# A mixture-of-state kernel on one Trainium2 core: contracting the first product over 256 (head, state) rows

## The chip, the cores and the metric

The kernel runs on one core of one Trainium2 chip. The metric is the device time of one execution in microseconds (us), median over several runs; for the kernel before it is 1129.18 us (three runs, 1129.02 to 1129.24). Besides, one execution was recorded by the hardware profiler, and all durations below come from that one.

## The reference, cut to what matters

Inputs are `x` (8 batches, 8 heads, 512 tokens, 64 features), `state` (8 batches, 8 heads, 32 states, 64 features), both in float32, and `w_in` (512 x 2048) and `w_out` (2048 x 512), both in float64. The output is float32.

```python
scores = scale * x @ state.T                 # per batch and head: 512 x 32
a      = softmax(scores, over the 32 states)
xread  = a @ state                           # 512 x 64
a2     = softmax(scores.T, over the 512 tokens)
sread  = a2 @ x                              # 32 x 64
rows   = concat([xread, sread], over tokens) # 8*544 rows of 8*64 = 512 features
h      = rows @ w_in                         # 4352 x 2048
out    = (h * erf(softplus(h))) @ w_out      # 4352 x 512
```

So a token's row before the first product is `xread`, for each head a weighted mean of that head's 32 states; the rows of the states themselves (`sread`, 32 for each batch) follow the tokens of their batch.

## The kernel before, in words

The work runs batch by batch. A batch has 512 tokens, and the hidden dimension of 2048 is cut into four groups g of 512 (`NG` = 4, each of `GF` = 4 tiles of 128). For each batch and group the kernel calls

- `hidden` (L219 to L236): for each of the four 128-wide tiles of the group, four matmuls (L230, k over the four 128-row blocks of the 512 features) accumulate `h` transposed, 128 x 512, in one of two PSUM buffers (`ps_h`); ScalarE writes softplus of it into `s` (L232), VectorE copies it into `hs` (L233); when all four are there ScalarE takes erf of `s` (L234) and VectorE multiplies with `hs` into `gT` (L235).
- `project` (L238 to L244): 16 matmuls (L241) add the group's share of the second product into four PSUM accumulators (`ps_o`), which after the last group are copied out by ScalarE (L249) and stored.

`project` of a group is called after `hidden` of the next one (`pending`). In the program every f32 matmul stands in the trace as two instructions, a transposing one as one.

`attention(b, hb, xx)` (L131 to L217) prepares the tokens of batch b for half of the heads (four heads in `hb`, in two pairs j). It is called twice for each batch, during the batch before it, after groups 1 and 3; for batch 0 it is called ahead of everything. Per half: the state block `st` is transposed (L136) to `stT`; x is transposed, 8 matmuls (L144), to `xT`; the token scores, 8 matmuls of 64 columns (L152); a softmax over states (L158 to L167, VectorE with an exp on ScalarE at L162); the state scores, two matmuls whose 64 output rows lie side by side in one PSUM bank (L173); a softmax over tokens (L177 to L185, exp at L181); both weights transposed back (L189, L196) and copied by ScalarE; `xread` transposed, two matmuls of 64 contraction rows each (L204), copied into `xx` (L206), which `hidden` reads; `sread`, 8 matmuls of 64 columns (L212), copied into `sT` (L216). All PSUM tiles of attention share two buffers (`ps_at`). `st` holds each head's 64 features in one half of 128 columns and zeros in the other.

After the eight batches a ninth chunk takes the 256 state rows from `sT` through the same `hidden` and `project`.

The weights arrive as float64 and are turned into float32 by VectorE (`weight`, L84 to L113): 16 chunks of 128 x 1024 elements, seven VectorE instructions each, the raw words in the two buffers of the tag `hs` that `hidden` uses as well, loaded by SyncE's DMA queue (L93). `weights(g)` is called ahead of `hidden(0, g)`, so the conversion runs during batch 0.

No order is written out by hand beyond this: a scheduler places each engine's instructions by priority (the order of the program) and readiness by its own estimates, so that matmuls of `hidden` and `project` are put between the steps of `attention`. Each engine then runs its own list strictly in that order.

Of the kernel before, what the change touches and what calls it, by code (L numbers as in the profile page):

```python
# [8 lines left out]
F32 = mybir.dt.float32  # L9
# [7 lines left out]
def kernel(  # L17
# [7 lines left out]
):  # L25
    nc = tc.nc
# [3 lines left out]
    P = 128  # L30
    QH = 4
    NH = H // QH
# [7 lines left out]
    assert QH * Ns == P and 2 * D == P and d_model == H * D and S == 512  # L40
# [3 lines left out]
    xin = ctx.enter_context(tc.tile_pool(name="xin", bufs=3))  # L44
    att = ctx.enter_context(tc.tile_pool(name="att", bufs=1))
    small = ctx.enter_context(tc.tile_pool(name="small", bufs=2))
    xmid = ctx.enter_context(tc.tile_pool(name="xmid", bufs=2))
    act = ctx.enter_context(tc.tile_pool(name="act", bufs=2))
    act1 = ctx.enter_context(tc.tile_pool(name="act1", bufs=1))
# [8 lines left out]


    st = const.tile([P, NH, B, 2 * D], F32, name="st")  # L60
    nc.vector.memset(st, 0.0)

# [3 lines left out]
    def load_x(b, hb):  # L66
        t = xin.tile([P, NC, QH, D], F32, name="x")
        for q in range(QH):
            nc.sync.dma_start(out=t[:, :, q, :],  # L69
                              in_=x[b, QH * hb + q].rearrange("(p c) d -> p c d", c=NC))  # L70
        x_t[b, hb] = t

    load_x(0, 0)
    for hb in range(NH):
        for q in range(QH):
            nc.sync.dma_start(
                out=st[Ns * q:Ns * q + Ns, hb, :, D * (q % 2):D * (q % 2) + D],
                in_=state[:, QH * hb + q].rearrange("b n d -> n b d"))
    load_x(0, 1)
# [4 lines left out]
    def weight(dst, src, shape):  # L84
# [12 lines left out]
        e = act.tile([P, n], U32, name="u")  # L97
# [7 lines left out]
        m = act.tile([P, n], U32, name="s")  # L105
        nc.vector.tensor_scalar(m, hi, 0xFFFFF, 0x100000, op0=ALU.bitwise_and,
                                op1=ALU.bitwise_or)
        f = act1.tile([P, n], F32, name="w")
# [8 lines left out]
    def weights(g):  # L117
        fs = slice(gw * g, gw * g + gw)
        for k in range(0, NK, 2):
            weight(w_in[:, k:k + 2, fs],  # L120
                   moe_w_in[P * k:P * k + 2 * P, fs].rearrange("(k p) f -> p k f", p=P),
                   (2, gw))
        for t in range(GF * g, GF * g + GF, 2):
            weight(w_out[:, t:t + 2, :],
                   moe_w_out[P * t:P * t + 2 * P].rearrange("(t p) e -> p t e", p=P),
                   (2, d_model))


    sT = const.tile([P, NK, B, Ns], F32, name="sT")

    def attention(b, hb, xx):  # L131

        xt = x_t.pop((b, hb))

        stT_ps = ps_at.tile([P, P], F32, name="at")
        nc.tensor.transpose(out=stT_ps, in_=st[:, hb, b, :], identity=ident)  # L136
        stT = small.tile([P, P], F32, name="stT")
        nc.scalar.copy(stT, stT_ps)  # L138

        xT = att.tile([P, 2, S], F32, name="xT")  # L140
        for j in range(2):
            xp = ps_at.tile([P, S], F32, name="at")
            for c in range(NC):
                nc.tensor.transpose(out=xp[:, P * c:P * c + P],  # L144
                                    in_=xt[:, c, 2 * j:2 * j + 2, :], identity=ident)
            nc.scalar.copy(xT[:, j, :], xp)  # L146


        s1 = ps_at.tile([P, NC, QH, Ns], F32, name="at")
        for c in range(NC):  # L150
            for j in range(2):
                nc.tensor.matmul(out=s1[:, c, 2 * j:2 * j + 2, :],  # L152
                                 lhsT=xT[:, j, P * c:P * c + P],
                                 rhs=stT[:, 2 * Ns * j:2 * Ns * j + 2 * Ns],
                                 start=True, stop=True)
        s1v = s1.rearrange("p c q n -> p (c q) n")
        m1 = small.tile([P, NC * QH], F32, name="m1")
        nc.vector.reduce_max(out=m1, in_=s1v, axis=AX.X)  # L158
        a = att.tile([P, NC * QH, Ns], F32, name="a")
        nc.vector.tensor_tensor(a, s1v, m1.unsqueeze(2).to_broadcast([P, NC * QH, Ns]),  # L160
                                op=ALU.subtract)
        nc.scalar.activation(out=a, in_=a, func=ACTF.Exp, scale=scale)  # L162
        z1 = small.tile([P, NC * QH], F32, name="z1")
        nc.vector.reduce_sum(out=z1, in_=a, axis=AX.X)
        nc.vector.tensor_scalar(z1, z1, 1e-9, None, op0=ALU.add)
        nc.vector.reciprocal(z1, z1)
        nc.vector.tensor_tensor(a, a, z1.unsqueeze(2).to_broadcast([P, NC * QH, Ns]),  # L167
                                op=ALU.mult)


        s2 = ps_at.tile([P, S], F32, name="at")
        for j in range(2):
            nc.tensor.matmul(out=s2[D * j:D * j + D, :],  # L173
                             lhsT=stT[:, 2 * Ns * j:2 * Ns * j + 2 * Ns],
                             rhs=xT[:, j, :], start=True, stop=True)
        m2 = small.tile([P, 1], F32, name="m2")
        nc.vector.reduce_max(out=m2, in_=s2, axis=AX.X)  # L177
        nc.vector.tensor_scalar(m2, m2, -scale, None, op0=ALU.mult)
        a2 = att.tile([P, S], F32, name="a2")
        z2 = small.tile([P, 1], F32, name="z2")  # L180
        nc.scalar.activation(out=a2, in_=s2, func=ACTF.Exp, bias=m2, scale=scale,  # L181
                             accum_out=z2)
        nc.vector.tensor_scalar(z2, z2, 1e-9, None, op0=ALU.add)
        nc.vector.reciprocal(z2, z2)
        nc.vector.tensor_scalar(a2, a2, z2, None, op0=ALU.mult)  # L185

        aT_ps = ps_at.tile([P, S], F32, name="at")
        for c in range(NC):
            nc.tensor.transpose(out=aT_ps[:, P * c:P * c + P],  # L189
                                in_=a[:, QH * c:QH * c + QH, :], identity=ident)  # L190
        aT = att.tile([P, S], F32, name="aT")
        nc.scalar.copy(aT, aT_ps)  # L192

        a2T_ps = ps_at.tile([P, NC, P], F32, name="at")
        for c in range(NC):
            nc.tensor.transpose(out=a2T_ps[:, c, :], in_=a2[:, P * c:P * c + P],  # L196
                                identity=ident)
        a2T = att.tile([P, NC, P], F32, name="a2T")
        nc.scalar.copy(a2T, a2T_ps)

        for j in range(2):
            rows = slice(2 * Ns * j, 2 * Ns * j + 2 * Ns)
            y = ps_at.tile([P, S], F32, name="at")
            nc.tensor.matmul(out=y, lhsT=st[rows, hb, b, :], rhs=aT[rows, :],  # L204
                             start=True, stop=True)
            nc.scalar.copy(xx[:, 2 * hb + j, :], y)  # L206


        sr = ps_at.tile([P, 2, 2 * Ns], F32, name="at")
        for j in range(2):  # L210
            for c in range(NC):
                nc.tensor.matmul(out=sr[:, j, :], lhsT=xt[:, c, 2 * j:2 * j + 2, :],  # L212
                                 rhs=a2T[:, c, 2 * Ns * j:2 * Ns * j + 2 * Ns],
                                 start=(c == 0), stop=(c == NC - 1))
        for e in range(2):
            nc.scalar.copy(sT[D * e:D * e + D, 2 * hb:2 * hb + 2, b, :],  # L216
                           sr[D * e:D * e + D, :, Ns * e:Ns * e + Ns])  # L217

    def hidden(xx, n, g):  # L219

        hs = act.tile([P, GF, S], F32, name="hs")[:, :, 0:n]
        s = act.tile([P, GF, S], F32, name="s")[:, :, 0:n]
        gT = act.tile([P, GF, S], F32, name="gT")[:, :, 0:n]
        for i in range(GF):
            f0 = P * (GF * g + i)
            hp = ps_h.tile([P, S], F32, name="h")
            for k in range(NK):
                nc.tensor.matmul(out=hp[:, 0:n], lhsT=w_in[:, k, f0:f0 + P], rhs=xx[:, k, :],  # L230
                                 start=(k == 0), stop=(k == NK - 1))
            nc.scalar.activation(out=s[:, i, :], in_=hp[:, 0:n], func=ACTF.Softplus)  # L232
            nc.vector.tensor_copy(hs[:, i, :], hp[:, 0:n])  # L233
        nc.scalar.activation(out=s, in_=s, func=ACTF.Erf)  # L234
        nc.vector.tensor_tensor(gT, s, hs, op=ALU.mult)  # L235
        return gT  # L236
# [28 lines left out]
    def new_xx():  # L265
        return xmid.tile([P, NK, S], F32, name="xx")

    xx = new_xx()
    for hb in range(NH):
        attention(0, hb, xx)  # L270

    chunks = [(S, put_x(b)) for b in range(B)] + [(B * Ns, put_s)]
    pending = None
    for b, (n, put) in enumerate(chunks):
        nxt = new_xx() if b + 1 < B else None
        cur = xx if b < B else sT.rearrange("p k b n -> p k (b n)")
        acc = None
        for g in range(NG):
            if b + 1 < B and g % 2 == 0:
                load_x(b + 1, g // 2)  # L280
            if b == 0:
                weights(g)
            gT = hidden(cur, n, g)
# [9 lines left out]
            if b + 1 < B and g % 2 == 1:  # L293
                attention(b + 1, g // 2, nxt)
        xx = nxt
# [31 lines left out]
```

## Time and profile before

| what | us |
|---|---|
| median of three runs | 1129.18 |
| the profiled execution's own time | 1126.09 |
| its span, first to last instruction | 1124.3 |
| TensorE matmuls busy | 1084.4 |
| ScalarE busy, table loads included | 365.4 |
| VectorE busy | 334.7 |
| mean granted TensorE clock | 0.985 |

The page gives, for each engine, the time in which an instruction was running and its share of the span; then the chain of work that ended last, followed back from the last instruction. Each piece of the chain belongs to the engine and line that everything later waited for. A busy TensorE can be one that runs short matmuls in a row, so the length of a stretch and the count of matmuls in it are read together. In the names of rows, `128*64 128x512` is a matmul with 128 contraction rows, 64 output rows and 512 columns. PE is TensorE, PEld its weight loads, DVE VectorE, ACT ScalarE, SP SyncE.

### The profile page before, as it was taken

To read this page: it belongs to the slowest core of one execution; us is meant where nothing else is said; L and a number is where in the kernel's file an instruction comes from. 1 tells how busy PE (TensorE), PEld (TensorE's weight loads), DVE (VectorE), ACT (ScalarE), POOL (GpSimd) and SP (SyncE) were. 2 spreads that over 40 slices of the span, in tenths; PEclk is the share of its full clock that TensorE was granted. 3 is DMA by queue.
4 is the path that set the end of the run, shared out by engine and by line. 5 is a ranking of instruction groups with operands and counts; after the bars stand their busy time and mean duration, and the time that the engine had idled before them with its cause. 6 is when DMAs were issued, how large, how long until landed. Compare 5 with 4: busy or idle time off the path is not lost.

```text
span 1124.3 us, 7665 instructions
## 1 busy us (share of the span) xinstructions
PE 1084.4 (96%) x3152; PEld 530.1 (47%) x3152; DVE 334.7 (30%) x469; ACT 365.4 (33%) x494; POOL 0.7 (0%) x6
## 2 busy tenths in 40 slices
PE   6779999999999999999999999999999999999998
PEld 4434444454444445454444445454444445444564
DVE  2888873221222212221211312221211311211111
ACT  2143214432342413432342413432342413322242
POOL 0000000000000000000000000000000000000000
PEclk9589999999999999999999999999999999999999
DMA  5333331000010001000010001000000000000000
GB/s 162 100 112 129 117 109 29 29 19 1 1 56 1 19 1 29 28 15 5 0 57 0 20 1 29 28 4 15 1 35 3 1 0 10 29 0 1 19 19 19
DMA packets 45346, 35.09 MB, mean 31 GB/s; under 512 B 36864, under 2 KB 36864, under 8 KB 45312
## 3 DMA queue, kind: packets, MB, share of 16 engines
q1 hardware_dynamic: 45312, 34.61, 10.1%
q8 instruction: 25, 0.41, 0.2%
q14 instruction: 9, 0.07, 0.0%
HBM read 25.69 MB, written 8.91 MB: 31 GB/s over the span
## 4 chain that ended last, share of the span: by engine, by line
PE 94%; DVE 2%; ACT 2%; DMA 1%; SPq 0%; issue 0%; ACTq 0%
PE h L230 42%; PE o L241 41%; PE at L212 3%; PE at L152 3%; PE at L204 2%; PE at L144 2%; PE at L173 1%; ACT xx L206 1%; PE at L196 1%; PE at L189 1%; DMA hs<-in_moe_w_in_dram 0%; ACT s L234 0%; DVE u L102 0%; ACT L234 0%; SPq L69 0%
## 5 line engine op out<-in xcount | busy, mean ns | idle before, releaser
L241 PE MATMUL o<-w_out,gT 128*128 128x512 f32 x1088 | 477.6, 592 | 0.7 <-DVE gT L235 0.7
L230 PE MATMUL h<-xx,w_in 128*128 128x512 f32 x1024 | 460.1, 600 | 6.7 <-DVE w_in L111 6.6
L241 PEld LDWEIGHTS o<-w_out,gT 128*128 128x128 f32 x1088 | 206.1, 190 | 254.5 <-issue 252.6
L230 PEld LDWEIGHTS h<-xx,w_in 128*128 128x128 f32 x1024 | 192.3, 192 | 243.3 <-issue 230.0
L233 DVE COPY hs<-h 128x512 f32<-128x512 f32 (+1 forms) x144 | 95.2, 661 | 518.0 <-ACT s L232 518.0
L232 ACT ACTIVATE s<-h 128x512 f32<-128x512 f32 (+1 forms) x144 | 82.2, 573 | 403.9 <-PE h L230 403.5
L235 DVE TENSOR_TENSOR gT<-s,hs 128x2048 f32<-128x2048 f32 (+1 forms) x36 | 78.2, 2173 | 78.6 <-ACT s L234 78.6
L234 ACT ACTIVATE s<-s 128x2048 f32<-128x2048 f32 (+1 forms) x36 | 65.3, 1815 | 0.4
L232 ACT ACT_TABLE_LOAD x37 | 47.5, 1283 | 42.1 <-DVE w L109 41.5
L158 DVE TENSOR_REDUCE m<-at 128x16 f32<-128x512 f32 x16 | 11.1, 691 | 160.0 <-PE at L152 160.0
L138 ACT COPY stT<-at 128x128 f32<-128x128 f32 x16 | 4.2, 265 | 131.9 <-PE at L136 131.8
L234 ACT ACT_TABLE_LOAD x36 | 46.2, 1283 | 0.6
L212 PE MATMUL at<-a2T,x 128*128 128x64 f32 x256 | 33.6, 287 | 9.2 <-ACT xx L206 9.2
L212 PEld LDWEIGHTS at<-a2T,x 128*128 128x128 f32 x256 | 31.4, 200 | 23.4 <-ACT xx L206 23.4
L152 PEld LDWEIGHTS at<-stT,xT 128*128 128x128 f32 x256 | 34.3, 209 | 8.3 <-ACT xT L146 5.4
L152 PE MATMUL at<-stT,xT 128*128 128x64 f32 x256 | 34.9, 292 | 0.6 <-ACT xT L146 0.5
L249 ACT COPY ot<-o 128x512 f32<-128x512 f32 x34 | 19.8, 582 | 45.9 <-PE o L241 45.9
L230 PE MATMUL h<-sT,w_in 128*128 128x256 f32 x128 | 28.9, 379 | 0.0
L230 PEld LDWEIGHTS h<-sT,w_in 128*128 128x128 f32 x128 | 24.3, 190 | 6.7 <-issue 3.8
L192 ACT COPY aT<-at 128x512 f32<-128x512 f32 x16 | 9.4, 585 | 42.1 <-PE at L189 42.1
L204 PE MATMUL at<-aT,st 64*128 64x512 f32 x64 | 21.5, 694 | 0.9 <-ACT aT L192 0.9
L144 PE MATMUL at<-ident,x 128*128 128x128 f32 x128 | 20.6, 297 | 1.3 <-ACT stT L138 0.9
(44 smaller groups left out, 354.4 us busy)
## 6 DMA issues: line engine op xcount, KB each, us to landing
x<-in_x_dram SPq DMA_DIRECT2D x64, 128.0 KB, 2.9
hs<-in_moe_w_in_dram SPq DMA_DIRECT2D x8, 1024.0 KB, 5.3
hs<-in_moe_w_out_dram SPq DMA_DIRECT2D x8, 1024.0 KB, 4.9
out_dram<-ot SPq DMA_DIRECT2D x32, 256.0 KB, 2.2
st<-in_state_dram SPq DMA_DIRECT2D x8, 64.0 KB, 2.3
out_dram<-ot SPq DMA_DIRECT2D x8, 64.0 KB, 1.7
```

The source lines that it names most:

```text
L144: nc.tensor.transpose(out=xp[:, P * c:P * c + P], in_=xt[:, c, 2 * j:2 * j + 2, :], identity=ident)
L152: nc.tensor.matmul(out=s1[:, c, 2 * j:2 * j + 2, :], lhsT=xT[:, j, P * c:P * c + P], rhs=stT[:, 2 * Ns * j:2 * Ns * j + 2 * Ns], start=Tru ...
L173: nc.tensor.matmul(out=s2[D * j:D * j + D, :], lhsT=stT[:, 2 * Ns * j:2 * Ns * j + 2 * Ns], rhs=xT[:, j, :], start=True, stop=True)
L204: nc.tensor.matmul(out=y, lhsT=st[rows, hb, b, :], rhs=aT[rows, :], start=True, stop=True)
L212: nc.tensor.matmul(out=sr[:, j, :], lhsT=xt[:, c, 2 * j:2 * j + 2, :], rhs=a2T[:, c, 2 * Ns * j:2 * Ns * j + 2 * Ns], start=(c == 0), stop ...
L230: nc.tensor.matmul(out=hp[:, 0:n], lhsT=w_in[:, k, f0:f0 + P], rhs=xx[:, k, :], start=(k == 0), stop=(k == NK - 1))
L232: nc.scalar.activation(out=s[:, i, :], in_=hp[:, 0:n], func=ACTF.Softplus)
L233: nc.vector.tensor_copy(hs[:, i, :], hp[:, 0:n])
L234: nc.scalar.activation(out=s, in_=s, func=ACTF.Erf)
L235: nc.vector.tensor_tensor(gT, s, hs, op=ALU.mult)
L241: nc.tensor.matmul(out=acc[r], lhsT=gT[:, i, P * r:P * r + P], rhs=w_out[:, GF * g + i, :], start=(g == 0 and i == 0), stop=(g == NG - 1 a ...
L249: nc.scalar.copy(ot, acc[r])
```

## The change

A token's row is a (weights over states) times state, so the first product can be written as a times (state @ w_in): per batch there are 8 x 32 = 256 rows (head, state) of state @ w_in, and `hidden` contracts over those 256 rows in place of the 512 features.

- `mixed(b, g)` is new: it makes the 256 x 512 block of state @ w_in of a batch and group, as eight matmuls of 64 contraction rows (one head's features), 32 output rows (its states) and 512 columns. The heads with even number (e = 0) use the contraction rows 0 to 63 and one PSUM bank, the odd ones rows 64 to 127 and the other bank; the four pairs i lie in different 32-row strips of the bank. One half is copied out by ScalarE and one by VectorE. It is called for batch b + 1 after each group of batch b, for batch 0 right after the group's `w_in`.
- `hidden` takes a list of pairs: two matmuls per tile for the tokens (`mg`, `aT`), four as before for the state rows.
- `attention(b)` is called once for each batch, after group 1, for all eight heads. The state scores are eight matmuls laid out like those of `mixed`; ScalarE copies them out, and the token scores are made from them by eight transposes in place of the matmuls of L152. The matmuls of L204 and the copies into `xx` are gone: `aT` is what `hidden` reads. `sread` is 32 matmuls with 32 output rows and 64 columns, its normalisation moved behind it, and one more transpose puts it into `sT`.
- `st` has no zero halves any more and isn't cleared; x of a batch is loaded with eight DMAs at group 0; the state's DMAs come after all of x of batch 0.
- `weight` works in one tile of the tag `s` (three buffers, before two) for its two temporaries, and `hidden` writes its product over `s`; the tags `u`, `w`, `gT` and the `xx` buffers are gone. `weights(g)` is split, with `mixed(0, g)` between the halves.

```diff
-    def attention(b, hb, xx):
+    def states(b):
+        ps = ps_at.tile([P, P], F32, name="at")
+        nc.tensor.transpose(out=ps, in_=st[:, b, :], identity=ident)
+        stT[b] = keep.tile([P, P], F32, name="stT")
+        nc.scalar.copy(stT[b], ps)
+
+    def attention(b):
+        xt = x_t.pop(b)
...
+        s2 = [ps_at.tile([P, S], F32, name="at") for _ in range(2)]
+        for i in range(NI):
+            for e in range(2):
+                r, q = slice(D * e, D * e + D), slice(Ns * i, Ns * i + Ns)
+                nc.tensor.matmul(out=s2[e][q, :], lhsT=stT[b][r, q], rhs=xT[r, i, :],
                                  start=True, stop=True)
...
+        sc = att.tile([P, 2, S], F32, name="sc")
+        for e in range(2):
+            nc.scalar.copy(sc[:, e], s2[e])
...
+            s1 = ps_at.tile([P, NC * NI, Ns], F32, name="at")
+            for c in range(NC):
+                nc.tensor.transpose(out=s1[:, NI * c:NI * c + NI, :],
+                                    in_=sc[:, e, P * c:P * c + P], identity=ident)
...
-        for j in range(2):
-            rows = slice(2 * Ns * j, 2 * Ns * j + 2 * Ns)
-            y = ps_at.tile([P, S], F32, name="at")
-            nc.tensor.matmul(out=y, lhsT=st[rows, hb, b, :], rhs=aT[rows, :],
-                             start=True, stop=True)
-            nc.scalar.copy(xx[:, 2 * hb + j, :], y)
...
+        sr = ps_at.tile([P, 2, D], F32, name="at")
+        for e in range(2):
+            for c in range(NC):
+                for i in range(NI):
+                    q = slice(Ns * i, Ns * i + Ns)
+                    nc.tensor.matmul(out=sr[q, e, :], lhsT=a2T[:, e, c, q],
+                                     rhs=xt[:, c, 2 * i + e, :],
+                                     start=(c == 0), stop=(c == NC - 1))
...
+    def mixed(b, g):
+        mg = mix.tile([P, 2, gw], F32, name="m")
+        ps = [ps_at.tile([P, gw], F32, name="at") for _ in range(2)]
+        for i in range(NI):
+            for e in range(2):
+                r, q = slice(D * e, D * e + D), slice(Ns * i, Ns * i + Ns)
+                nc.tensor.matmul(out=ps[e][q, :], lhsT=stT[b][r, q],
+                                 rhs=w_in[r, i, gw * g:gw * g + gw], start=True, stop=True)
+        nc.scalar.copy(mg[:, 0], ps[0])
+        nc.vector.tensor_copy(mg[:, 1], ps[1])
+        m_t[b, g] = mg
...
-            for k in range(NK):
-                nc.tensor.matmul(out=hp[:, 0:n], lhsT=w_in[:, k, f0:f0 + P], rhs=xx[:, k, :],
-                                 start=(k == 0), stop=(k == NK - 1))
+            for k, (lhsT, rhs) in enumerate(pairs):
+                nc.tensor.matmul(out=hp[:, 0:n], lhsT=lhsT[:, P * i:P * i + P], rhs=rhs,
+                                 start=(k == 0), stop=(k == len(pairs) - 1))
...
-            if b + 1 < B and g % 2 == 0:
-                load_x(b + 1, g // 2)
             if b == 0:
-                weights(g)
-            gT = hidden(cur, n, g)
+                weights_in(g)
+                mixed(0, g)
+                weights_out(g)
+            if b + 1 < B and g == 0:
+                load_x(b + 1)
+                states(b + 1)
+            gT = hidden(pairs(b, g), n)
...
-            if b + 1 < B and g % 2 == 1:
-                attention(b + 1, g // 2, nxt)
+            if b + 1 < B:
+                mixed(b + 1, g)
+                if g == 1:
+                    attention(b + 1)
```

More of the change, by code (lines that the diff above doesn't have):

```diff
@@ L30 @@
     P = 128
-    QH = 4
-    NH = H // QH
+    NI = H // 2
     NC = S // P
@@ L56, with load_x @@
     make_identity(nc, ident)
-    st = const.tile([P, NH, B, 2 * D], F32, name="st")
-    nc.vector.memset(st, 0.0)
     x_t = {}
[L66 to L79, printed above, removed]
+    def load_x(b):
+        t = xin.tile([P, NC, H, D], F32, name="x")
+        for h in range(H):
+            nc.sync.dma_start(out=t[:, :, h, :], in_=x[b, h].rearrange("(p c) d -> p c d", c=NC))
+        x_t[b] = t
+    load_x(0)
+    st = const.tile([P, B, P], F32, name="st")
+    for h in range(H):
+        i, e = h // 2, h % 2
+        nc.sync.dma_start(out=st[Ns * i:Ns * i + Ns, :, D * e:D * e + D],
+                          in_=state[:, h].rearrange("b n d -> n b d"))
     w_in = const.tile([P, NK, d_ff], F32, name="w_in")
@@ L95, in weight @@
         lo, hi = words[:, :, 0], words[:, :, 1]
-        e = act.tile([P, n], U32, name="u")
+        em = act.tile([P, 2, n], U32, name="s", bufs=3)
+        e, m = em[:, 0], em[:, 1]
         nc.vector.tensor_scalar(e, hi, 20, 0x7FF, op0=ALU.logical_shift_right,
@@ L115, with weights_in @@
     gw = GF * P
-    def weights(g):
+    def weights_in(g):
         fs = slice(gw * g, gw * g + gw)
@@ L129 @@
     sT = const.tile([P, NK, B, Ns], F32, name="sT")
-    def attention(b, hb, xx):
[L133 to L140, printed above, removed]
-        for j in range(2):
+    stT = {}
+    aT = {}
+    def states(b):
[3 more added lines that the diff above has]
+        nc.scalar.copy(stT[b], ps)
@@ L142, in attention @@
+    def attention(b):
+        xt = x_t.pop(b)
+        xT = att.tile([P, NI, S], F32, name="xT")
+        for i in range(NI):
             xp = ps_at.tile([P, S], F32, name="at")
             for c in range(NC):
[L144 to L154, printed above, removed]
-                                 start=True, stop=True)
@@ L156, in attention @@
[L156 to L182, printed above, removed]
+                nc.tensor.transpose(out=xp[:, P * c:P * c + P], in_=xt[:, c, 2 * i:2 * i + 2, :],
+                                    identity=ident)
@@ new lines, in attention @@
+        a = att.tile([P, 2, NC * NI, Ns], F32, name="a")
+        a2 = att.tile([P, 2, S], F32, name="a2")
+        a2T = att.tile([P, 2, NC, P], F32, name="a2T")
+        aT[b] = keep.tile([P, 2, S], F32, name="aT")
+        z2 = small.tile([P, 2], F32, name="z2")
+        for e in range(2):
[3 more added lines that the diff above has]
+                                    in_=sc[:, e, P * c:P * c + P], identity=ident)
+            m1 = small.tile([P, NC * NI], F32, name="m1")
+            nc.vector.reduce_max(out=m1, in_=s1, axis=AX.X)
+            nc.vector.tensor_tensor(a[:, e], s1, m1.unsqueeze(2).to_broadcast([P, NC * NI, Ns]),
+                                    op=ALU.subtract)
+            m2 = small.tile([P, 1], F32, name="m2")
+            nc.vector.reduce_max(out=m2, in_=sc[:, e], axis=AX.X)
+            nc.vector.tensor_scalar(m2, m2, -scale, None, op0=ALU.mult)
+            nc.scalar.activation(out=a[:, e], in_=a[:, e], func=ACTF.Exp, scale=scale)
+            nc.scalar.activation(out=a2[:, e], in_=sc[:, e], func=ACTF.Exp, bias=m2, scale=scale,
+                                 accum_out=z2[:, e:e + 1])
+            z1 = small.tile([P, NC * NI], F32, name="z1")
+            nc.vector.reduce_sum(out=z1, in_=a[:, e], axis=AX.X)
+            nc.vector.tensor_scalar(z1, z1, 1e-9, None, op0=ALU.add)
+            nc.vector.reciprocal(z1, z1)
+            nc.vector.tensor_tensor(a[:, e], a[:, e],
+                                    z1.unsqueeze(2).to_broadcast([P, NC * NI, Ns]), op=ALU.mult)
@@ new lines, in attention @@
+        for e in range(2):
+            ps = ps_at.tile([P, NC, P], F32, name="at")
+            for c in range(NC):
+                nc.tensor.transpose(out=ps[:, c, :], in_=a2[:, e, P * c:P * c + P],
+                                    identity=ident)
+            nc.scalar.copy(a2T[:, e], ps)
+        for e in range(2):
+            ps = ps_at.tile([P, S], F32, name="at")
+            for c in range(NC):
+                nc.tensor.transpose(out=ps[:, P * c:P * c + P],
+                                    in_=a[:, e, NI * c:NI * c + NI, :], identity=ident)
+            nc.vector.tensor_copy(aT[b][:, e], ps)
@@ L183, in attention @@
         nc.vector.tensor_scalar(z2, z2, 1e-9, None, op0=ALU.add)
         nc.vector.reciprocal(z2, z2)
[L185 to L194, printed above, removed]
@@ L219, in hidden @@
-    def hidden(xx, n, g):
+        sr = ps_at.tile([P, 2, D], F32, name="at")
+        for e in range(2):
+            for c in range(NC):
+                for i in range(NI):
[3 more added lines that the diff above has]
+                                     start=(c == 0), stop=(c == NC - 1))
+        sn = small.tile([P, 2, D], F32, name="sn")
+        for e in range(2):
+            nc.vector.tensor_scalar(sn[:, e], sr[:, e], z2[:, e:e + 1], None, op0=ALU.mult)
@@ new lines, in attention @@
+        ps = ps_at.tile([P, NI, Ns], F32, name="at")
+        nc.tensor.transpose(out=ps, in_=sn, identity=ident)
+        nc.scalar.copy(sT[:, :, b, :], ps)
+    m_t = {}
+    def mixed(b, g):
+        mg = mix.tile([P, 2, gw], F32, name="m")
+        ps = [ps_at.tile([P, gw], F32, name="at") for _ in range(2)]
+        for i in range(NI):
+            for e in range(2):
+                r, q = slice(D * e, D * e + D), slice(Ns * i, Ns * i + Ns)
[4 more added lines that the diff above has]
+        m_t[b, g] = mg
@@ L234, in hidden @@
         nc.scalar.activation(out=s, in_=s, func=ACTF.Erf)
[L235 to L236 removed]
+        nc.vector.tensor_tensor(s, s, hs, op=ALU.mult)
+        return s
     def project(gT, n, g, acc):
@@ L263, in put_s, with pairs @@
             nc.sync.dma_start(out=out[r0:r0 + Ns], in_=ot[Ns * j:Ns * j + Ns, :])
[L265 to L270, printed above, removed]
+    def pairs(b, g):
+        if b < B:
+            mg = m_t.pop((b, g))
+            return [(mg[:, e], aT[b][:, e]) for e in range(2)]
+        return [(w_in[:, k, gw * g:gw * g + gw], sT[:, k].rearrange("p b n -> p (b n)"))
+                for k in range(NK)]
+    states(0)
+    attention(0)
     chunks = [(S, put_x(b)) for b in range(B)] + [(B * Ns, put_s)]
```

34 lines of the change are left out of this document (9 added, 25 removed).

## The prediction

> **What bounds the kernel now.** I read the page first, for which engine the end hangs on.
>
> ```profile
> span 1124.3 us, 7665 instructions
> ...
> PE 1084.4 (96%) x3152; PEld 530.1 (47%) x3152; DVE 334.7 (30%) x469; ACT 365.4 (33%) x494; POOL 0.7 (0%) x6
> ...
> PE 94%; DVE 2%; ACT 2%; DMA 1%; SPq 0%; issue 0%; ACTq 0%
> ```
>
> TensorE is busy 96% and carries 94% of the chain. Whether it is busy with the products or with attention decides what shorter products are worth, so the groups come next, different shapes kept apart.
>
> ```profile
> L241 PE MATMUL o<-w_out,gT 128*128 128x512 f32 x1088 | 477.6, 592 | 0.7 <-DVE gT L235 0.7
> L230 PE MATMUL h<-xx,w_in 128*128 128x512 f32 x1024 | 460.1, 600 | 6.7 <-DVE w_in L111 6.6
> ```
>
> The first product of the tokens takes 460 us in 1024 instructions: two for each matmul of the program (8 batches x 4 groups x 4 tiles x 4 = 512). The third view is the chain in order of time, over one batch.
>
> ```profile
> 373.02 2.00 PE at L212 x16
> 375.02 6.92 PE h L230 x16
> 381.94 13.73 PE o L241 x32
> 395.67 13.73 PE h L230 x32
> ...
> 423.25 1.01 PE at L144 x8
> 424.26 0.86 PE h L230 x2
> 425.12 1.73 PE at L152 x16
> 426.85 1.01 PE at L173 x4
> ...
> 433.21 0.44 PE at L189 x4
> 433.64 0.44 PE at L196 x4
> 434.08 0.86 PE o L241 x2
> 434.94 1.11 PE at L204 x4
> 436.05 0.57 ACT xx L206
> ...
> 500.32 2.00 PE at L212 x16
> ```
>
> From one second-half L212 to that of the next batch is 127.30 us. 32 instructions of 512 columns take 13.73 us, 0.429 each, in `hidden` and `project` alike; a batch has 128 of each, 109.8 us. The other 17.5 us are the two halves of attention, every step of which stands on TensorE's own chain, with one wait of about 0.6 us per half (for the copy at L206). In this regime whatever TensorE no longer does comes off the time. The fourth view, the stretches, shows where that is not so.
>
> ```profile
> core 0: us, PE busy (x) PEld busy (x) DVE busy (x) ACT busy (x) POOL busy (x), PEclk, DMA share, GB/s
> 0.00:47.00 47.00, 30.17 (x114) 21.35 (x115) 21.13 (x37) 11.98 (x23) 0.70 (x6) 0.77 0.43 123
> 47.00:177.30 130.30, 120.46 (x324) 55.60 (x324) 109.35 (x141) 38.80 (x51) 0.00 (x0) 0.95 0.35 113
> 813.80:941.10 127.30, 125.96 (x372) 60.25 (x371) 28.65 (x42) 43.05 (x58) 0.00 (x0) 1.00 0.02 9
> 941.10:1050.93 109.83, 109.16 (x275) 49.41 (x274) 20.24 (x20) 33.54 (x39) 0.00 (x0) 1.00 0.03 10
> 1050.93:1124.30 73.37, 68.83 (x225) 42.21 (x223) 11.70 (x20) 22.75 (x33) 0.00 (x0) 1.00 0.07 22
> ```
>
> I cut the run so that each stretch of a batch starts where that batch's `hidden` starts and the last `project` of the batch before is still to do: batch 0 to 177.3, six batches of 127.3, the last one without attention 109.8 (four groups of 27.46), and the state rows 73.4. Sum 1124.3. ScalarE (43 of 127) and VectorE (29) are far from full in a steady batch; in batch 0 VectorE is at 109 of 130, converting weights. So batch 0 has a second limit close behind the first.
>
> **The tokens' product.** Two matmuls per tile for four: 64 instructions less per batch x 0.429 = 27.46 us saved in each of the eight.
>
> **The price of the small matmuls.** `mixed` has eight matmuls of 64 contraction rows and 32 output rows, 16 instructions of 512 columns. One after another they would take 16 x 0.429 = 6.87 us, four such blocks 27.5 per batch, and nothing would be won. Do matmuls that occupy different parts of the array run at once? The timeline of TensorE shows two kinds that do.
>
> ```profile
> 363.13 1.08 PE L173 MATMUL at<-xT,stT 128*64 128x512 f32 x4
> 364.14 0.70 PE L230 MATMUL h<-xx,w_in 128*128 128x512 f32 x1
> ```
>
> L173 has two matmuls with 64 output rows each in different halves of one bank: four instructions, and the next line starts 1.01 us after them; in a row they would need 1.72. L204, with two halves of the contraction rows and two banks, takes 1.11 on the chain. So both ways of splitting run two at once: two slots of 0.429 and some 0.15 to 0.25 for emptying the array on either side. The new blocks split both ways, 2 x 4 parts, each part used by one matmul. If all eight run at once a block again takes two slots: 0.86 + 0.25 + a few hundredths, 1.15 us. Bounds: 1.0 (L173's), and 6.9 (no overlap). I take 1.15, since the rows show each split by itself at full overlap, and four-fold splitting is more of the second kind. The Trainium skill, in "TensorE: Matmul & The Clock Gate", Part 3, says that matmuls of different array tiles run together, but also that matmuls start and end strictly in program order. The trace agrees with the first (1.01 us above). The second would hold the next part's first instruction behind its neighbour's second one, three slots (1.29 us) for L173 where 1.01 was measured; what that order would do to eight parts is a rival below.
>
> **Attention, per batch, by the chain's rows.** Gone: L152 (2 x 1.73), L173 (2 x 1.01), L204 (2 x 1.1), L212 (2 x 2.00), the two waits on L206 (1.2). Transposes: 34 before, 42 after (16 of x, 8 each of scores, a and a2, one of the state, one of `sread`) at 0.11 (0.44 for four): 4.6 us. Scores: one block, 1.15. The new `sread` is 64 instructions of 64 columns, four parts at once: 16 slots of 0.11 to 0.125 (2.00 / 16) are 2.0, with emptying 2.2; without overlap 7 to 8. Mixed: 4 x 1.15 = 4.6. The chain from scores to `aT` is now one long one instead of two short ones: copy, transposes, maximum, subtraction, exp, sum, reciprocal, product, transposes, copy, twice over with two shared PSUM buffers. The cover is `hidden` of group 2 and `project` of group 1 (6.9 + 13.7 us), placed between as before; without it the chain would cost some 10 to 15 us, from copies and VectorE steps of 0.6 to 0.7 us each. With it I put 3 us for handovers that miss, against about 1.5 now; bounds 1 and 10.
>
> Steady batch: 27.5 + 54.9 + 4.6 + 1.15 + 4.6 + 2.2 + 3 = 98.0 us (before 127.3). Last batch 82.4, state rows 73.4 unchanged.
>
> **Batch 0.** Here VectorE becomes the limit.
>
> ```profile
> 12.85 1.13 SPq L93 DMA_DIRECT2D hs<-in_moe_w_in_dram  x2
> ...
> 31.59 0.68 DVE L98 TENSOR_SCALAR u<-hs 128x1024 uint32<-128x1024 uint32 x1
> 32.19 0.68 DVE L160 TENSOR_TENSOR a<-at,m 128x512 f32<-128x512 f32 x1
> ...
> 36.21 1.21 DVE L102 SCALAR_TENSOR_TENSOR u<-hs,u 128x1024 uint32<-128x1024 uint32 x1
> 37.34 0.68 DVE L167 TENSOR_TENSOR a<-a,z 128x512 f32<-128x512 f32 x1
> ```
>
> Starts are 0.60 apart behind the short kind and 1.13 behind the long; a chunk (four short, three long) takes 5.8 us, the four chunks of a group 23.3. Add per group the four copies at L233 (2.4), the product at L235 (2.2), two copies of `mixed` (1.2) and a quarter of attention's 8.5 us: 31.2. The raw words share two buffers with `hidden`, and a load takes about 5 us after a buffer comes free, so I add 2 of waiting: 33 per group, bounds 31 and 37. The x of batch 1 now queues behind these loads on SP; attention(1) comes after group 1, so it has time. TensorE needs only 6.9 + 13.7 + 2.3 + 2.1 = 25 per group, so its saving there is covered. The gain is an earlier start: the first load is issued at 12.85 and its conversion starts at 31.59, behind a VectorE step that waited for the second half's scores. That half is gone, so conversion can start when the words land, about 16.5 (x and state take 16 issues on SP, fewer than the 20 ahead of that load now). Group 0 is converted at 16.5 + 8.5 + 23.3 + 2 = 50, group 3 at 50 + 99 = 149, when by then the `project` of group 3 and the next `hidden` are to do: my cut at 150, before 177.3. Bounds 140 and 165.
>
> **The sum.** 150 + 6 x 98.0 + 82.4 + 73.4 = 893.8 us of span. The profiled execution took 1126.09, 1.8 over its span; the median is 1129.18, 4.9 over the span. So 898.7, and I forecast 898. The case's own range, from 140 and 96 per batch to 165 and 102: 877 to 933.
>
> **The rivals.**
>
> *Only neighbours overlap.* If two of eight run at once, a block takes eight slots, 3.7 us, and a batch 5 x 2.55 + 1.5 (`sread`) more: 112.3; batch 0 stays near 152. 152 + 674 + 82.4 + 73.4 + 4.9 = 987. For it: the trace shows two at once and never more. Against: nothing there shows two as a limit. By the skill's strict order a block takes nine slots, 4.1 us: about 1000.
>
> *The products' buffers become the pace.* A tile of `hidden` now takes 1.72 us for 3.43, and there are two buffers.
>
> ```profile
> 522.81 5.74 PE L230 MATMUL h<-xx,w_in 128*128 128x512 f32 x13
> ...
> 526.45 0.60 ACT L232 ACTIVATE s<-h 128x512 f32<-128x512 f32 x1 [12.05 <-PE h L230]
> ...
> 527.08 0.69 DVE L233 COPY hs<-h 128x512 f32<-128x512 f32 x1 [11.65 <-ACT s L232]
> ```
>
> The eighth instruction starts at 522.81 + 3.00; softplus starts 0.64 later, the copy follows it and ends at 527.77, 1.96 after that start. With four instructions per tile the buffer is free 1.29 + 1.96 = 3.25 us after its first instruction and wanted again at 3.43. That is 0.18 of room. A table load of 1.28 between erf and softplus, pushed behind the copy of `mixed` that ScalarE now has in its list, would cost up to 1.1 per group, 35 us in all: 935 to 945.
>
> *Slower.* If matmuls of 64 x 32 parts don't overlap at all (four streams out of the same contraction rows is what no row shows), a block costs 7.1 and `sread` 7.2: a batch 98 + 5 x 5.95 + 5 = 132.8. Batch 0 is then TensorE's again: per group 6.9 + 13.7 + 2 x 7.1 + 4.7 = 39.5, from 45 on to 203. 203 + 797 + 82.4 + 73.4 + 4.9 = 1161. It turns slower from about 6 us per block. Against it stand L173 and L204, each fully overlapped.
>
> *The change does nothing like this:* the counts of matmuls are written in the program, so I leave it out.
>
> **How the numbers follow.** All eight at once 0.72 (877 to 933), neighbours only 0.12 (about 990), the buffers' pace 0.11 (933 to 960), no overlap 0.05 (1161). Range 872 to 960: the first and third cases, 0.83. Three runs agree within 0.02%, and a measurement can tell some 0.2% from no change. Faster 0.94, same 0.01, slower 0.05.
>
> **What would show it.** Right: 512 instructions of the tokens' `hidden` at 0.43; each block of 16 followed by another line some 1.1 us after its start; 98 us from batch to batch; VectorE over 90% busy until about 150. Blocks of 2, 3.7 or 7 us prove the overlap wrong; blocks of 1.1 with batches over 102 put the fault into waits for PSUM buffers, shown before the third tile of `hidden` or inside attention.

## The result, and the profile after

The changed kernel takes 895.04 us (median of four runs, 890.89 to 896.08) against 1129.1 for the kernel before on the same chip: a ratio of 0.7921, 95% interval 0.7893 to 0.7949. The forecast was 898. The profiled execution took 890.89 us with a span of 889.1; it is the fastest of the four, so the sums below, made against its span, stand some 4 us under the median.

The page of the kernel after, its engines and its chain:

```profile
span 889.1 us, 7809 instructions
...
PE 835.7 (94%) x3216; PEld 378.6 (43%) x3216; DVE 354.9 (40%) x500; ACT 351.7 (40%) x460; POOL 0.7 (0%) x6
...
PE 83%; DVE 11%; DMA 3%; SPq 1%; ACT 1%; issue 0%; DVEq 0%
```

TensorE has 64 instructions more than before and is busy 249 us less. Its share of the chain has fallen from 94% to 83%; VectorE and loads now hold 14%, and the stretches show where.

```profile
core 0: us, PE busy (x) PEld busy (x) DVE busy (x) ACT busy (x) POOL busy (x), PEclk, DMA share, GB/s
0.00:47.00 47.00, 23.58 (x163) 11.74 (x163) 29.27 (x49) 12.79 (x23) 0.70 (x6) 0.78 0.63 168
47.00:164.30 117.30, 93.17 (x374) 36.94 (x375) 103.06 (x135) 34.55 (x47) 0.00 (x0) 0.93 0.36 117
638.50:733.40 94.90, 94.90 (x379) 42.03 (x379) 31.49 (x47) 41.52 (x55) 0.00 (x0) 1.00 0.03 12
733.40:815.81 82.41, 82.41 (x193) 36.49 (x193) 20.88 (x21) 31.46 (x34) 0.00 (x0) 1.00 0.03 13
815.81:889.10 73.29, 68.83 (x225) 42.21 (x223) 11.70 (x20) 22.74 (x33) 0.00 (x0) 1.00 0.07 22
```

The cut is that of the prediction: a stretch starts where a batch's `hidden` starts with the last `project` of the batch before still to do, found by counting back from the state rows. Batch 0 ends at 164.3 (before 177.3), a steady batch takes 94.85 us (before 127.30), the last 82.4 (109.8), the state rows 73.3 as before. In the steady batch shown (638.50 to 733.40) TensorE is busy without a gap; in batch 0 it is busy for 117 of 164 us, and VectorE for 132.

Of the groups, the tokens' product and the mixed rows (busy us, mean ns of one):

```profile
L246 PE MATMUL h<-aT,m 128*128 128x512 f32 x512 | 240.4, 606 | 6.5 <-DVE hs L249 6.5
...
L231 PE MATMUL at<-w_in,stT 64*32 64x512 f32 x512 | 43.2, 629 | 4.0 <-DVE w_in L108 3.7
```

Half the instructions of the tokens' product are gone; in their place stand as many small ones that take 43 us in all. How, TensorE's timeline shows (start, duration):

```profile
301.61 1.09 PE L231 MATMUL at<-w_in,stT 64*32 64x512 f32 x16
302.63 0.70 PE L246 MATMUL h<-aT,m 128*128 128x512 f32 x1
```

Sixteen instructions of 512 columns, and the next line starts 1.02 us after the first of them. A narrower window holds the first half of the same block:

```profile
301.61 0.66 PE L231 MATMUL at<-w_in,stT 64*32 64x512 f32 x8
```

Eight instructions start and end within 0.66 us, hardly longer than the 629 ns that one of them lasts on the mean: eight instructions run at once, one on each of the eight parts of the array, and then the eight second ones do. That the two instructions of one part follow each other is read from these times; the run with four parts below bears it out. The chain of one batch, in order of time, from one L155 towards the next:

```profile
308.08 1.24 PE at L155 x16
...
319.33 1.03 PE at L212 x64
320.36 1.05 PE o L257 x2
...
330.97 1.02 PE at L231 x16
331.99 3.63 PE h L246 x8
335.62 1.72 PE o L257 x4
337.34 3.43 PE h L246 x8
340.77 12.02 PE o L257 x28
...
402.93 1.24 PE at L155 x16
```

It is one unbroken row of matmuls; no copy stands in it, where two copies at L206 stood in each batch of the kernel before. One thing is easily overlooked: the eight instructions of `hidden` right behind a block of small matmuls take 3.63 us, and 3.43 elsewhere. So a block costs 1.02 us and 0.20 more in the products behind it.

### The profile page after: what moved, and what is told of

It reads as the page before. It is cut to its first block, busy times and chain, and to the rows that moved or that the text cites. A ratio compares the mean times of both kernels' runs of the same rounds, so it can differ in the third digit from the quotient of the medians.

```text
span 889.1 us, 7809 instructions
## 1 busy us (share of the span) xinstructions
PE 835.7 (94%) x3216; PEld 378.6 (43%) x3216; DVE 354.9 (40%) x500; ACT 351.7 (40%) x460; POOL 0.7 (0%) x6
## 4 chain that ended last, share of the span: by engine, by line
PE 83%; DVE 11%; DMA 3%; SPq 1%; ACT 1%; issue 0%; DVEq 0%
PE o L257 49%; PE h L246 26%; PE at L231 3%; DMA hs<-in_moe_w_in_dram 3%; DVE s L106 2%; DVE s L100 2%; PE at L145 1%; DVE s L96 1%; DVE s L103 1%; DVE s L98 1%; PE at L212 1%; PE at L155 1%; PE at L199 1%; PE at L193 1%; DVE w_in L108 1%; DVE s L251 1%
## 5 line engine op out<-in xcount | busy, mean ns | idle before, releaser
L257 PE MATMUL o<-w_out,s 128*128 128x512 f32 x1088 | 488.8, 597 | 15.1 <-DVE s L251 15.1
L257 PEld LDWEIGHTS o<-w_out,s 128*128 128x128 f32 x1088 | 204.0, 191 | 260.9 <-issue 241.7
L246 PE MATMUL h<-aT,m 128*128 128x512 f32 x512 | 240.4, 606 | 6.5 <-DVE hs L249 6.5
L246 PEld LDWEIGHTS h<-aT,m 128*128 128x128 f32 x512 | 93.9, 192 | 131.2 <-issue 116.9
L251 DVE TENSOR_TENSOR s<-s,hs 128x2048 f32<-128x2048 f32 (+1 forms) x36 | 78.2, 2173 | 74.7 <-ACT s L250 74.7
L233 ACT COPY m<-at 128x512 f32<-128x512 f32 x32 | 18.7, 585 | 210.0 <-PE at L231 210.0
L234 DVE COPY m<-at 128x512 f32<-128x512 f32 x32 | 22.1, 689 | 166.4 <-PE at L231 166.4
L231 PE MATMUL at<-w_in,stT 64*32 64x512 f32 x512 | 43.2, 629 | 4.0 <-DVE w_in L108 3.7
L147 ACT COPY xT<-at 128x512 f32<-128x512 f32 x32 | 17.4, 590 | 7.3 <-PE at L145 7.3
L106 DVE SCALAR_TENSOR_TENSOR s<-hs,s 128x1024 f32<-128x1024 uint32 x16 | 19.5, 1218 | 0.1
```

Of the source, the lines that this page charges most:

```text
L106: nc.vector.scalar_tensor_tensor(out=f, in0=lo, scalar=2.0 ** -32, in1=m, op0=ALU.mult, op1=ALU.add)
L231: nc.tensor.matmul(out=ps[e][q, :], lhsT=stT[b][r, q], rhs=w_in[r, i, gw * g:gw * g + gw], start=True, stop=True)
L234: nc.vector.tensor_copy(mg[:, 1], ps[1])
L246: nc.tensor.matmul(out=hp[:, 0:n], lhsT=lhsT[:, P * i:P * i + P], rhs=rhs, start=(k == 0), stop=(k == len(pairs) - 1))
L251: nc.vector.tensor_tensor(s, s, hs, op=ALU.mult)
L257: nc.tensor.matmul(out=acc[r], lhsT=gT[:, i, P * r:P * r + P], rhs=w_out[:, GF * g + i, :], start=(g == 0 and i == 0), stop=(g == NG - 1 a ...
```

## The experiments

The kernel before measured 1127.23 and 1126.84 us in the two groups of runs below and 1129.1 beside the changed kernel, so ratios to it are compared as well as times.

**Three buffers for the raw words.** Batch 0 ended 14 us later than forecast, and VectorE was waiting for loads there.

```diff
-    mix = ctx.enter_context(tc.tile_pool(name="mix", bufs=6))
+    mix = ctx.enter_context(tc.tile_pool(name="mix", bufs=4))
...
-        raw = act.tile([P, 2 * n], U32, name="hs")
+        raw = act.tile([P, 2 * n], U32, name="hs", bufs=3)
...
-        hs = act.tile([P, GF, S], F32, name="hs")[:, :, 0:n]
+        hs = act.tile([P, GF, S], F32, name="hs", bufs=3)[:, :, 0:n]
```

> The changed kernel with three buffers for the tag of the raw weight words and of hidden's copy (two before), paid for with four buffers of the mixed rows for six. Theory: batch 0 ends at 164.3 us and not at 150 because a load of raw words is issued only when a buffer comes free and then takes 5 us; with a third buffer about 2 to 3 us per group come back, some 10 us in all: 880 to 886. Rival: VectorE's own work sets batch 0 (132 us busy of 164); then the time stays within 3 us of 895.

884.88 us (884.68 to 885.72), ratio 0.7855 (0.7830 to 0.7881): 10 us by the medians, as in the theory, 7.5 by the ratios and 6.2 between the two profiled spans. VectorE's idle time ahead of the first step of a conversion, in the kernel after and in this one (what ended the wait: us, times):

```profile
  DMA hs<-in_moe_w_in_dram: 22.7, 5
```

```profile
  DMA hs<-in_moe_w_in_dram: 15.7, 1
```

One wait is left, for the very first load; the four others, 7 us in all, are gone, and batch 0 ends at 158.1.

**Batch 0's copies on ScalarE.**

```diff
-        nc.vector.tensor_copy(mg[:, 1], ps[1])
+        (nc.scalar.copy if b < 2 else nc.vector.tensor_copy)(mg[:, 1], ps[1])
...
-            nc.vector.tensor_copy(hs[:, i, :], hp[:, 0:n])
+            (nc.scalar.copy if b == 0 else nc.vector.tensor_copy)(hs[:, i, :], hp[:, 0:n])
...
```

> The changed kernel with the copies of hidden's products in batch 0, and the second copy of each mixed block made during batch 0, on ScalarE in place of VectorE. Theory that VectorE's work and its strict order set batch 0: six copies of 0.6 us less on VectorE per group, 14 us, and hidden's buffers no longer wait behind a conversion: 877 to 885. Rival, the loads of raw words alone set it: the loads still come 5 us after a buffer is free, so less than 4 us are gained.

887.05 us (886.14 to 888.67), ratio 0.7876 (0.7845 to 0.7908): 8 us by the medians, 5 by the ratios, between the two theories and short of the first. The same view says why:

```profile
  DMA hs<-in_moe_w_in_dram: 29.7, 5
  DMA hs<-in_moe_w_out_dram: 2.1, 1
```

Without the one long wait at the start (15.7 in the run above), 16 us of waiting for loads stand where 7 stood. VectorE got through its list sooner and waited longer for the loads. So neither limit explains batch 0 alone: the work and the loads alternate.

**Both together.**

> The changed kernel with both edits of the first two runs: three buffers for the raw words, and in batch 0 the copies of hidden's products and of the mixed rows on ScalarE. Theory: each edit alone left the other limit (with three buffers VectorE waits for no load any more, with fewer copies it waits 14.0 us for loads in place of 7.3), so together they give more than the sum of 10 and 8 us or at least the sum: 870 to 878. Rival, that TensorE's own work sets batch 0 by then: 882 to 885, no better than three buffers alone.

875.46 us (874.45 to 876.62), ratio 0.7770 (0.7749 to 0.7791): 19.6 us by the medians (17 by the ratios), at least the sum of the two (18.2; 12.5 by the ratios), and the fastest version that computes everything. Batch 0 ends at 150.0.

**One conversion step less on top of it.** The edit leaves out the clamping of exponents outside float32's range:

```diff
-        nc.vector.tensor_scalar(e, e, -896.0, 0.0, op0=ALU.add, op1=ALU.max)
-        nc.vector.tensor_scalar(e, e, 255.0, 8388608.0, op0=ALU.min, op1=ALU.mult)
+        nc.vector.tensor_scalar(e, e, -896.0, 8388608.0, op0=ALU.add, op1=ALU.mult)
```

> The kernel of the run before with six VectorE instructions per chunk of weights in place of seven: it leaves out the clamping of exponents outside float32's range. Theory that VectorE's work is what is left of batch 0's limit: 16 x 0.60 = 9.6 us less than the run before. Rival, that loads or TensorE set it: less than 3 us less.

874.34 us (873.34 to 874.67): 1.1 us, the rival's case; my theory failed here. From 40 to 152 us the engines of the run before and of this one:

```profile
40.00:152.00 112.00, 98.77 (x404) 39.83 (x401) 96.34 (x120) 52.95 (x79) 0.00 (x0) 0.91 0.36 122
```

```profile
40.00:152.00 112.00, 99.44 (x405) 39.48 (x404) 86.83 (x106) 53.03 (x78) 0.00 (x0) 0.92 0.37 122
```

VectorE (third of the engines) is busy 9.5 us less, TensorE (first) as long as before, at a mean granted clock of 0.91 to 0.92. With both edits a further cut in VectorE's work no longer shortens batch 0. The two profiles show two things that stand instead. In this window VectorE's wait for one load grew from 1.6 to 6.9 us. And in both runs TensorE waits twice, 5.7 us each time, for the product of erf and `hs` (11.4 us in all): that wait is a table load, erf and the product in a row behind `hidden`, which the edit doesn't touch. What TensorE's lowered clock costs beside that wasn't tested.

**No parts.** The mixed rows by matmuls on the whole array:

```diff
+    stz = [const.tile([P, NI, 2, P], F32, name="stz%d" % v) for v in range(2)]
...
-                nc.tensor.matmul(out=ps[e][q, :], lhsT=stT[b][r, q],
-                                 rhs=w_in[r, i, gw * g:gw * g + gw], start=True, stop=True)
+                nc.tensor.matmul(out=ps[e], lhsT=stz[b % 2][:, i, e, :],
+                                 rhs=w_in[:, i, gw * g:gw * g + gw],
+                                 start=(i == 0), stop=(i == NI - 1))
```

> The changed kernel with the mixed rows made by eight matmuls on the whole array (state padded with zeros to 128 x 128, accumulated over the four pairs), so that no two can run at once; eight more small ScalarE copies per batch and four buffers of mixed rows. Theory that the side-by-side parts carry the gain: a block costs 16 x 0.429 = 6.9 us and not 1.02, a steady batch 94.9 + 4 x 5.85 = 118.3, so 140 us more over six batches and 20 to 45 more in batch 0, where TensorE becomes the limit again: 1055 to 1080. Rival, that the small products lie in time that TensorE has idle anyway: less than 20 us more.

1047.43 us (1045.75 to 1048.92), ratio 0.9296 (0.9265 to 0.9328). The chain, with the same block in two successive batches at first and last:

```profile
617.98 6.87 PE at L237 x16
624.85 3.43 PE h L253 x8
...
736.44 6.87 PE at L237 x16
```

A block costs 6.87 and a batch 118.46, as the theory had them, and the products behind a block take 3.43 again: the 0.20 more stands only behind blocks that use parts. The total missed its range by 8 us on the low side, for the most part because batch 0 grew by 14 and not by 20 to 45 (the rest is that the profiled execution of the kernel after lies 4 us under its median): of the 47 us that eight blocks add there (8 x 5.85), most fell into time in which TensorE was waiting. Two thirds of the change's gain, 152 of 234 us, hang on the parts.

**Four parts.**

```diff
+    stz = [const.tile([P, 2, P], F32, name="stz%d" % v) for v in range(2)]
...
-                nc.tensor.matmul(out=ps[e][q, :], lhsT=stT[b][r, q],
-                                 rhs=w_in[r, i, gw * g:gw * g + gw], start=True, stop=True)
+                nc.tensor.matmul(out=ps[e][q, :], lhsT=stz[b % 2][:, e, q],
+                                 rhs=w_in[:, i, gw * g:gw * g + gw], start=True, stop=True)
```

> The changed kernel with the mixed rows made by matmuls of 128 contraction rows (the other head's rows zero) and 32 output rows: four parts of the array with two matmuls each in place of eight parts with one; two more small copies per batch, four buffers of mixed rows. Theory that a block's time is the number of instructions on one part times 0.43 us: four slots, 1.9 us for 1.02, a steady batch 94.85 + 4 x 0.86 = 98.3, and 20 to 28 us in all: 912 to 925. Rival, that a block's price is switching and emptying the array, whatever the number of parts: within 5 us of 895.

916.77 us (916.25 to 919.01), ratio 0.8144 (0.8123 to 0.8164). The chain again, over one batch:

```profile
538.04 1.87 PE at L237 x16
560.71 1.88 PE at L237 x16
...
636.31 1.88 PE at L237 x16
```

98.27 us per batch, 3.42 more for four blocks: 0.86 each, two slots of 0.43 and nothing besides. With 1.02, 1.87 and 6.87 us for eight parts, four parts and one, the block's time is 0.43 times the instructions that share a part, plus about 0.15 where the array is used in parts, and the 0.20 behind it.

**The old contraction under the new attention.** No mixed rows; `xread` from `aT` by parts of 32 x 64, `hidden` over the 512 features:

```diff
+            for v in range(2):
+                i = 2 * h + v
+                q = slice(Ns * i, Ns * i + Ns)
+                for e in range(2):
+                    nc.tensor.matmul(out=ys[v][D * e:D * e + D, :],
+                                     lhsT=st[q, b, D * e:D * e + D], rhs=aT[b][q, e, :],
+                                     start=True, stop=True)
...
-            mg = m_t.pop((b, g))
-            return [(mg[:, e], aT[b][:, e]) for e in range(2)]
...
+        return [(w_in[:, k, gw * g:gw * g + gw],
+                 xx[b][:, k] if b < B else sT[:, k].rearrange("p b n -> p (b n)"))
+                for k in range(NK)]
```

> The changed kernel's attention with the contraction of before: xread made from aT by matmuls of 32 contraction and 64 output rows, hidden over 512 features, no mixed rows. Theory: per batch 27.5 us more in hidden, 4.1 less for the mixed blocks, some 2.5 more for xread: a steady batch of 121, six of them 156 us more, the last batch 27.5 and batch 0 about 10 more: 1080 to 1095, so that the rewritten attention alone is worth 35 to 50 us against the kernel before. Rival, that the rewritten attention gives most of the gain: under 1000.

1087.65 us (1087.56 to 1088.47), ratio 0.9655 (0.9625 to 0.9686). What this version keeps (the rewritten attention, and the other order of loads and conversions in batch 0) is worth 40 us, the contraction over the states another 193. Cut as above, some 17 of the 40 us lie in batch 0 and 22 in the six steady batches. The chain from one score block to that of the next batch:

```profile
591.81 1.02 PE at L156 x16
...
604.74 0.59 ACT xx L215
...
606.50 0.59 ACT xx L215
...
607.14 1.71 PE at L226 x64
608.85 2.01 PE h L245 x2
...
715.03 1.02 PE at L156 x16
```

A batch takes 123.2, two more than expected. The chain has some 3 us in it that the kernel after doesn't have: two waits of 0.66 us for the copy of `xread`, and behind them `sread` in 1.71 us for 1.03 and two instructions of `hidden` in 2.01 for 1.06, at a granted clock of 0.62 from 607 to 611.5. Batch 0 ends at 160.6, 3.7 earlier than in the kernel after, where some 10 later was expected. So the total lies in its range because two misses cancel.

## Why the prediction was right, point by point

The mechanism held, and two terms were mis-sized in opposite directions: batch 0 was 14.3 us over, six steady batches 19 us under. That the total came within 4 us is luck.

- *What bounds the kernel:* held. What TensorE no longer does came off the steady batches in full.
- *The tokens' product:* held. 512 instructions where 1024 stood, and 27.4 us less in the last batch, which has nothing else that changed.
- *The price of the small matmuls:* taken as 1.15 us by combining L173 and L204, measured 1.02, and 1.22 with what the products behind it lose. Four ways of one kind of splitting cost no more than two. The rivals "only neighbours overlap" and "slower" are excluded by that row and by the run with four parts. The rule of the Trainium skill ("TensorE: Matmul & The Clock Gate", Part 3) that matmuls start strictly in the program's order would have made 4.1 us of a block, by the prediction's estimate. This trace, with the eight first instructions inside 0.66 us and 1.02 in all, is against it if the two instructions of an f32 matmul stand side by side in TensorE's list, as the prediction took it; the trace lists instructions in order of time, so that order isn't shown. The Trainium skill's other statement there, that matmuls of different tiles run together, is borne out by the same rows.
- *Attention:* 98.0 per batch was 94.85. The new `sread` was taken at 2.2 us and took 1.03: I had carried over the 0.11 to 0.125 of a full-width matmul with 64 columns. The 3 us for handovers that miss didn't come: 94.85 less 82.4 for the products leaves 12.45, of which the blocks take 5.3, 42 transposes 4.9 and `sread` 1.0. The last 1.2 are the 0.2 us lost behind each of five blocks and behind `sread`; TensorE waits for no other engine there.
- *Batch 0:* the failed term. The start was as forecast (first conversion step at 15.43 us against 16.5, group 0 converted at 51 against 50, group 1 at 85 against 83). Group 2, which has attention's VectorE steps in its middle, took 40 us and not 33, so the last conversion ended at 158.6 and not at 149. From the end of group 0's conversion to there VectorE was busy 96.6 us and idle 11.1, where the forecast had 93 and 6: it counted three quarters of attention's 8.5 us where all of them fall, and "I add 2 of waiting" was too little. Part of what was missed is the order of VectorE's list, and the buffers of tag `s` that softplus shares with the conversions. In group 2, on ScalarE, VectorE and TensorE:

```profile
118.88 1.28 ACT L248 ACT_TABLE_LOAD   x1 [4.32 <-DVE w_out L108]
120.17 1.09 ACT L248 ACTIVATE s<-h 128x512 f32<-128x512 f32 x2
```

```profile
121.66 1.21 DVE L100 SCALAR_TENSOR_TENSOR s<-hs,s 128x1024 uint32<-128x1024 uint32 x1
122.80 0.68 DVE L249 COPY hs<-h 128x512 f32<-128x512 f32 x1
```

```profile
123.53 3.72 PE L246 MATMUL h<-aT,m 128*128 128x512 f32 x8 [3.27 <-DVE hs L249]
```

  The first two tiles of `hidden` were done at 118.2. Softplus began only after a conversion (L108) had freed a buffer of `s`; it was through with the first tile at about 120.8, and VectorE reached its copy at 122.80, behind a conversion step. TensorE, whose third tile needs that tile's PSUM buffer, stood idle for 3.27 us. Such waits are 6.5 us in batch 0; with the copies on ScalarE they are 1.4. The path to the end of batch 0 was another one than forecast, too. The chain there:

```profile
145.03 1.15 DVE w_in L108
146.22 1.06 PE at L231 x8
...
148.34 3.43 PE h L246 x8
151.77 5.15 PE o L257 x12
...
157.90 3.63 PE h L246 x8
```

  It goes from the last conversion of `w_in`, done at 146.2, to TensorE's own list (`hidden` of group 3 with `project` of group 2 between its tiles), and not through the last conversion of `w_out`. The forecast had this work done by the last conversion and the cut 1 us behind it; it came 5.7 behind. The two edits that take away the load waits and these copies brought the cut to 150.0.
- *The buffers' pace:* the condition is there, the cost isn't. ScalarE's timeline:

```profile
332.08 0.58 ACT L233 COPY m<-at 128x512 f32<-128x512 f32 x1 [9.46 <-PE at L231]
332.68 1.28 ACT L248 ACT_TABLE_LOAD   x1
333.98 0.60 ACT L248 ACTIVATE s<-h 128x512 f32<-128x512 f32 x1
```

  And VectorE's:

```profile
334.61 0.69 DVE L249 COPY hs<-h 128x512 f32<-128x512 f32 x1 [1.79 <-ACT s L248]
```

  The copy of the mixed rows does push the table load behind the start of `hidden` (331.99 on the chain above). But softplus follows the load at once, and VectorE's copy has freed the buffer at 335.30, before TensorE is through with the second tile at 335.62. Besides, the scheduler put four instructions of `project`, 1.72 us, between the second and third tile.
- *Sums and signs:* two sums are off by their own terms. The upper end of the range, 165 for batch 0 and 102 per batch, comes to 938 us with the 4.9 over the span, not 933; and 35 us on top of 898 are 933, not 935 to 945. Of the signs, VectorE "over 90% busy until about 150" was missed: it is busy 88% from 47 to 164 us.

## What to carry to other kernels

Cost a small matmul by the part of the array that it occupies: here a block lasted as long as the part with the most instructions, and some 0.35 us more. So split a set of small products over rows and columns before counting their number against them. When the engine that sets the end gets faster, look at the stage with a second limit close behind: here batch 0 became 13 us shorter where a steady batch became 32. And in that stage count what stands behind the long steps in the limiting engine's list, and what the other engines still have to do behind it, not only the sum of its work.

## What the runs showed of the hardware that I had not expected

64 instructions of 64 columns and 32 output rows took 1.03 us (four parts, 16 slots of 0.064), while the full-width ones of 64 columns in the kernel before took 16 slots in 2.00 us: the slot is little more than half as long. That the narrower weights do it wasn't tested. The changed kernel's runs spread over 5 us, and those of the kernel before over nearly 7 (1122.64 to 1129.42, fourteen runs), where four versions with a shorter batch 0 spread over 1 to 2.5; so the 0.02% of the first three runs was no measure of the spread. In batch 0 of the changed kernel the granted clock was 0.93 from 47 to 164 us and 1.00 in the stretches behind it; whether that makes the spread wasn't tried. With the old contraction the granted clock was 0.62 for 4.5 us behind two waits of 0.66 us (607 to 611.5). The kernel before has single waits of 0.67 us in the same place, and 1.00 behind them (436.5 to 442). What makes the difference is open.
